# An mLSTM cell feeding a mixture-of-depths layer: score rows through DRAM, and four moves in the order of work

## The chip, the cores and the metric

The kernel runs on one core of a Trainium2 chip. The metric is the device time of one execution in microseconds (us), less is better. A core has a matrix engine (PE, whose weight loads are listed as PEld), a vector engine (DVE), an activation engine (ACT), a general engine (POOL) and a queue engine (SP) that issues transfers. They run side by side and wait for one another through semaphores; each takes its own instructions in the order of the program.

## What is computed

Cut to what matters, with B=4 batches, H=8 heads, S=768 tokens, D=40 (so 320 numbers per token) and capacity 128:

```
per token t of each batch and head:
    m_new = max(f[t] + m, i[t])
    C = exp(f[t] + m - m_new) * C + exp(i[t] - m_new) * outer(v[t], k[t])
    n = exp(f[t] + m - m_new) * n + exp(i[t] - m_new) * k[t]
    y[t] = sigmoid(o[t]) * (C @ q[t]) / max(|n . q[t]|, 1)
x = y as rows of 320
scores = x @ w_gate                        # one per token
out = x
per batch: top = the 128 tokens with the highest scores
    out[top] = x[top] + sigmoid(scores[top]) * (relu(x[top] @ w1) @ w2)
```

## The kernel before, in words

The recurrence is done in chunks of L=128 tokens: six chunks (NT=6) for each of four batches, 24 steps in all, `step(n)` (L615). Within a chunk the tokens meet as an attention-like product; a state C carries what came before. The stages of step n are spread over the engines and over neighbouring steps:

- SP loads k, q, v and the output gate of chunk n+4 (L119 to L133, each 160 KB in pieces of 160 bytes; there are five buffers of each).
- PE turns k and q of chunk n+2 (L308), makes the scores of chunk n+1 (pS, L363), the product with the state (pIC, L389 and L395), and for chunk n the weighted sum pH (L420). ACT copies the turned tiles (L309), makes the gate weights W (L342) and the output gate (L319, L320). POOL masks W (L347), scales v (L354), the state (L377) and the gate by the normalizer, sor (L435). DVE multiplies P = pS * W (L369), adds the state's part to pH (L425), forms the normalizer (L429 to L433) and the result x = pH * sor (L440), which SP stores to the output (L441).
- pH has one buffer in PSUM: PE can begin pH of step n+1 only when DVE has read pH of step n for x.

Then comes the selection. `score` (L443) takes the dot product of each token with w_gate on DVE; the scores of a chunk stand in one column, one per partition. To rank the tokens of a batch each score is compared with all others. For that `spread` (L449) brings the column to all partitions as a row: a PE transpose of the broadcast column (pb, L452) and an ACT copy (sb, L453). `compare(u)` (L455) then compares on DVE the scores of chunk u with those of chunks 0 to u and writes ge and a count. Before the change, step n spreads chunk n-1 in its middle and compares it at its end. The first step of a batch (c=0) and the very last step do both "soon", in the middle of the step; the prologue has scores 0 and 1 both made ahead of step 2, which therefore spreads and compares two.

After a batch's last comparison PE sums ge (pcol, L466), DVE turns sums and counts into ranks (L479, L480) and into a one-hot matrix sel (L484), PE makes token numbers of it (pidx, L491), DVE writes them as integers (idx, L496) and POOL gathers the 128 chosen rows from the output in DRAM (xe, L498). One step later PE turns these rows (pX, L514), and the two layers (L534, L543) are dealt out in portions over the steps of the next batch; `leave` (L545) scatters the results. For batch 0 the ranking is in step 7, the gather at the head of step 8 and pX in step 9. The last batch's selection is the tail after step 23 (L828 to L878).

The order on each engine is the order in which the program's lines run: nothing is moved by a scheduler. All loads and stores named above are on SP's one queue. At the start there are nine filler matmuls (`warm`, L183, on a tile of ones made by DVE at L92), which use PE while nothing else is ready; then come the column ends (pe, L201), the mask of the first weights (`masked`, L322), the running maxima (pm, L213) and the gate operands (pO, L269), and then the first chunk's turn and weights.

Two terms of the code: tiles of one `tag` in a pool share its `bufs` buffers, and a tile that is still in use keeps its buffer; `[(ps_h, "h"), (ps_c, "c")]` says where `masked` puts its two halves. `T` tiles come through the two buffers of `ps_t`.

Of the kernel before, what the change touches and what calls it, by code (L numbers as in the profile page):

```python
# [8 lines left out]
FP = mybir.dt.float32  # L9
BF = mybir.dt.bfloat16  # L10
# [11 lines left out]
def kernel(  # L22
# [20 lines left out]
    nc = tc.nc  # L43

    B, H, S, D = q.shape
    L = 128
    NT = S // L
# [19 lines left out]
    const = ctx.enter_context(tc.tile_pool(name="const", bufs=1))  # L67
# [5 lines left out]
    ps_t = ctx.enter_context(tc.tile_pool(name="ps_t", bufs=2, space=PSUM))  # L73
# [2 lines left out]
    ps_h = ctx.enter_context(tc.tile_pool(name="ps_h", bufs=1, space=PSUM))  # L76
    ps_m = ctx.enter_context(tc.tile_pool(name="ps_m", bufs=2, space=PSUM))


    NR = 3 * BH  # L80
    f_sb = [gate.tile([NR, L], FP, name=f"f_sb{g}") for g in range(2)]
# [6 lines left out]

    load_gates(nc.sync, f_sb, f_gate, 0)
    load_gates(nc.scalar, i_sb, i_gate, 0)  # L90
    fill = const.tile([128, 4 * L], BF, name="fill")
    nc.vector.memset(fill, 1.0)  # L92

    unused = const.tile([1, 1], FP, name="unused")
# [88 lines left out]
    def warm(n):  # L183

        pw = ps_c.tile([128, 4 * L], FP, name="pw", tag="c")
        for _ in range(n):
            nc.tensor.matmul(pw, fill[:, 0:128], fill, start=True, stop=True)  # L187

    def sums(g, eng):

# [131 lines left out]
    def masked(pools):  # L322

        pW = [pool.tile([128, 4, L], FP, name="pW", tag=tag) for pool, tag in pools]
        for p in pW:
            nc.tensor.matmul(p, never, ident_b.unsqueeze(1).to_broadcast([128, 4, L]), start=True, stop=False)
        return pW
# [87 lines left out]
    def within(P, v1):  # L415
        pH = ps_h.tile([128, H, DP], FP, name="pH", tag="h")
        for j in range(2):
            for p in range(NP):
                for t in HALVES:
                    nc.tensor.matmul(pH[t, 2 * p + j, :], P[:, p, j, t], v1[:, 2 * p + j, :], start=True, stop=True)  # L420
        return pH

    def norm(num, pH, so):
        if num is not None:
            nc.vector.tensor_tensor(out=pH[:, :, 0:D1], in0=num, in1=pH[:, :, 0:D1], op=OP.add)  # L425
        num = pH

        den = work.tile([128, H], FP, name="den")
        nc.vector.scalar_tensor_tensor(out=den, in0=num[:, :, D], scalar=-2.0, in1=twos.to_broadcast([128, H]),  # L429
                                       op0=OP.mult, op1=OP.max)  # L430
        nc.vector.scalar_tensor_tensor(out=den, in0=num[:, :, D], scalar=2.0, in1=den, op0=OP.mult, op1=OP.max)
        rec = work.tile([128, H], FP, name="rec")
        nc.vector.reciprocal(out=rec, in_=den)  # L433
        sor = work.tile([128, H, D], FP, name="sor", bufs=2)
        nc.gpsimd.tensor_tensor(out=sor, in0=so, in1=rec.unsqueeze(2).to_broadcast([128, H, D]), op=OP.mult)  # L435
        return num, sor

    def result(b, c, num, sor):
        x = x_t[b, c] = work.tile([128, DM], FP, name="x", bufs=NT)
        nc.vector.tensor_tensor(out=x.rearrange("p (h d) -> p h d", d=D), in0=num[:, :, 0:D], in1=sor, op=OP.mult)  # L440
        nc.sync.dma_start(out=out[b, c * L:(c + 1) * L, :], in_=x)  # L441
# [7 lines left out]
    def spread(u, sc, sb):  # L449

        pb = ps_m.tile([128, L], FP, name="pb", tag="m")
        nc.tensor.transpose(pb, sc[:, u:u + 1].to_broadcast([128, L]), ident)  # L452
        nc.scalar.copy(out=sb[:, u, :], in_=pb)  # L453

    def compare(u, sc, sb, ge, cnt):  # L455


        n = (u + 1) * L
        nc.vector.scalar_tensor_tensor(out=ge[:, GE[u]:GE[u + 1]], in0=sb.rearrange("p t l -> p (t l)")[:, 0:n],  # L459
                                       scalar=sc[:, u:u + 1], in1=earlier[:, NT * L - n:],  # L460
                                       op0=OP.is_ge, op1=OP.mult, accum_out=cnt[:, u:u + 1])
# [25 lines left out]
    def number(sel, token):  # L487

        pidx = ps_m.tile([K_, 1], FP, name="pidx", tag="m")
        for t in range(NT):  # L490
            nc.tensor.matmul(pidx, sel[:, t, :], token[:, t:t + 1], start=(t == 0), stop=(t == NT - 1))  # L491
        return pidx

    def gather(b, pidx):
        idx = mod.tile([K_, 1], U32, name="idx")
        nc.vector.tensor_scalar(out=idx, in0=pidx, scalar1=float(b * S), scalar2=None, op0=OP.add)  # L496
        xe = xe_t[b % 2]
        nc.gpsimd.indirect_dma_start(out=xe[0:K_, 0:DM], out_offset=None, in_=rows(b),  # L498
                                     in_offset=bass.IndirectOffsetOnAxis(ap=idx, axis=0),
                                     bounds_check=(b + 1) * S - 1, oob_is_err=False)  # L500
        return idx, xe
# [63 lines left out]
    N = len(steps)  # L565
    T, W, wv, state = {}, {}, {}, {}
    layers, sel, picked, x_t = {}, {}, {}, {}
    P, pS, nums = {}, {}, {}
    hidden = {0, 1, 2, 3}

    def load(n):
        if n < N:
            load_qk(n)
            load_v(n)
            load_so(n)
# [35 lines left out]
    def run(hooks):  # L611
        for f in hooks:
            f()

    def step(n, **more):  # L615
        b, c = steps[n]
        _, v1, so = loaded[n]
        pb, pc = steps[n - 1]
        load(n + AHEAD)
        pH = within(P[n], v1)  # L620
        if n == NT + 1:
            pcol = columns_of(state[0][1][2])
        elif n == NT + 2:
            picked[0] = gather(0, number(sel[0], token))
        elif n == NT + 3:
            enter(0)

        soon = c == 0 or n == N - 1
        if n + 1 < N:
            decay(*steps[n + 1])  # L630
            hide(n + 1)
            give = exchange(*steps[n + 1], loaded[n + 1][0], T[n + 1], wv[n + 1])
            if n + 1 not in pS:
                pS[n + 1] = products(T[n + 1])
        if soon:
            spread(pc, *state[pb][1][:2])
        if c == 0:
            state[b] = open_batch()

        num, sor = norm(nums.get(n), pH, so)  # L640
        if n + 1 < N:
            nums[n + 1] = exchanged(*steps[n + 1], *give)
            if n + 1 not in P:
                P[n + 1] = weighted(pS[n + 1], W[n + 1])
        if soon:
            if c == 0:
                result(b, c, num, sor)
            compare(pc, *state[pb][1])
        if n == NT + 1:
            ranked(0, pcol)  # L650
        if n + 2 < N:
            stated(n + 2)
        run(more.get("places", ()))
        if n < NT + 3:

            turned(n + 2)
            run(more.get("spread", ()))
            if not soon:
                spread(pc, *state[pb][1][:2])
            copies = operands(*((0, 5) if n == 2 else (1, n - 3)), [(ps_m, "m")])  # L660
            W[n + 2] = weights(*steps[n + 2])
            run(copies)
        else:
            if n + 2 < N:
                W[n + 2] = weights(*steps[n + 2])
                hide(n + 2)
            layer(b, c)
            if c == 1:
                picked[b - 1] = gather(b - 1, number(sel[b - 1], token))
            elif c == 2:  # L670
                enter(b - 1)
            if n + 2 < N:
                turned(n + 2)
            if c == 0:
                pcol = columns_of(state[b - 1][1][2])
            elif not soon:
                spread(pc, *state[pb][1][:2])
        if n + 2 < N:
            gated(n + 2)
        if c > 0:  # L680
            result(b, c, num, sor)
        score(b, c, state[b][0])
        run(more.get("end", ()))
        if not soon:
            compare(pc, *state[pb][1])
        if b > 1 and c == 0:
            ranked(b - 1, pcol)
        elif n == NT + 3 or (b > 1 and c == 2):
            layers[b - 1].gate()
            if b > 1:  # L690
                layers[b - 2].leave()
# [8 lines left out]
    load_so(AHEAD - 1)  # L700
    load(AHEAD)
    nc.sync.dma_start(out=wg, in_=moe_w_gate.rearrange("(o d) -> o d", o=1).to_broadcast([128, DM]))
    warm(9)

    sums(0, nc.vector)
    maxima(0)
# [1 line left out]
    for n in range(1, 4):  # L708
        pads(n, nc.gpsimd)
    ends(0)  # L710
    pW = masked([(ps_h, "h"), (ps_c, "c")])
    split(0, 0, nc.vector, slice(0, BH))
    carry(0)
    pm = carried(0)
# [73 lines left out]
    keep(1, columns(1))  # L788
    stated(3)
    score(0, 0, state[0][0])  # L790
    score(0, 1, state[0][0])

    def second_places():
        for j in range(2):
            nc.gpsimd.memset(place[j][1], 0.0)
        places(1)

    gated(3)
    step(2, places=[second_places], spread=[lambda: spread(0, *state[0][1][:2])],
         end=[lambda: compare(0, *state[0][1])])  # L800
    for n in range(3, N):
        step(n)
        if n == 3:
# [24 lines left out]
    b, u = steps[-1]  # L828
# [76 lines left out]
```

## Time and profile before

| | |
|---|---|
| time, median of 3 executions | 189.27 us (188.05 to 191.15) |
| profiled execution: own time, span from first to last instruction | 193.54 us, 191.8 us |
| PE, DVE, POOL, ACT busy | 179.0, 139.8, 101.4, 99.9 us |
| chain that ended last: PE, waiting for nothing shown, DVE, POOL, DMA | 65%, 11%, 11%, 7%, 3% |
| SP's transfers | 105008 pieces, 22.50 MB |

The share of busy time is an average over stages with different limits: up to about 24 us the start with its ramp, from 30 to 62 us a stretch where DVE has hardly a pause, 62 to 75 us the first ranking, 75 to 166 us PE without a pause, then the tail. The chain of waits goes back from the last instruction and names at each step what released it. "x8" after a line of the chain says how many instructions were merged.

### The profile page before, as it was taken

What the parts mean: (1) busy time and instruction counts of PE and PEld (TensorE: products, weight loads), DVE (VectorE), ACT (ScalarE), POOL (GpSimd) and SP (SyncE); (2) the same over time, 40 slices, a digit from 0 to 9 for tenths busy, and PEclk for the clock granted to TensorE, in tenths of its full rate; (3) what the DMA queues carried; (4) which work ended last, traced back from release to release, by engine and by line L of the source; (5) the groups of instructions that cost most, each with busy time, mean ns of one, the idle gap of its engine ahead of it and who ended that gap; (6) DMA issues with size and microseconds to landing.
All of it is one profiled execution on the core that took longest, in us unless ns stands there. A gap on an engine that the chain in (4) does not pass through costs nothing.

```text
span 191.8 us, 6510 instructions
## 1 busy us (share of the span) xinstructions
PE 179.0 (93%) x2594; PEld 149.8 (78%) x2594; DVE 139.8 (73%) x413; ACT 99.9 (52%) x233; POOL 101.4 (53%) x171
## 2 busy tenths in 40 slices
PE   6999999789999887999999999999999999989990
PEld 2577888677877775989878889798788898859960
DVE  7633748988999868867899778868997788585101
ACT  3054466589898678466734473567344734201110
POOL 7954356597676639413774657327746571023202
PEclk9999999999999999999999999999999999999999
DMA  4999996597998999999999498597993101010100
GB/s 79 140 156 148 145 171 100 108 173 151 198 223 180 164 224 251 170 172 183 159 172 143 98 166 152 104 188 120 147 127 83 39 34 38 36 38 36 34 0 34
DMA packets 105854, 24.37 MB, mean 127 GB/s; under 512 B 100640, under 2 KB 105248, under 8 KB 105824
## 3 DMA queue, kind: packets, MB, share of 16 engines
q1 hardware_dynamic: 105008, 22.50, 74.0%
q0 software_dynamic: 384, 1.31, 2.2%
q8 instruction: 20, 0.33, 0.8%
q10 hardware_dynamic: 432, 0.15, 0.7%
q14 instruction: 10, 0.08, 0.2%
HBM read 19.37 MB, written 4.59 MB: 125 GB/s over the span
## 4 chain that ended last, share of the span: by engine, by line
PE 65%; issue 11%; DVE 11%; POOL 7%; DMA 3%; ACT 1%; POOLq 1%; ACTq 0%
PE pS L363 11%; PE pH L420 10%; PE pt L308 10%; PE ph L534 9%; PE py L543 5%; PE pIC L389 4%; PE pIC L395 4%; PE pW L341 3%; DVE P L369 3%; POOL W L347 3%; PE pw L187 2%; DMA out_dram<-ye,idx 2%; DMA xe<-out_dram,idx 2%; DVE ge L459 1%; POOL sor L435 1%
## 5 line engine op out<-in xcount | busy, mean ns | idle before, releaser
L342 ACT ACTIVATE W<-pW 128x512 f32<-128x512 f32 x48 | 26.1, 595 | 24.6 <-PE pW L341 15.2
L435 POOL TENSOR_TENSOR sor<-so,rec 128x320 f32<-128x320 f32 x24 | 17.8, 740 | 39.1 <-DVE rec L433 32.8
L347 POOL TENSOR_SCALAR_AFFINE_SELECT W<-W 128x512 f32<-128x512 f32 x46 | 32.0, 718 | 10.9 <-ACT W L342 10.9
L369 DVE TENSOR_TENSOR P<-pS,W 128x512 f32<-128x512 f32 x48 | 30.9, 685 | 7.6 <-PE pS L363 3.7
L309 ACT COPY T<-pt 128x512 f32<-128x512 f32 x47 | 25.5, 589 | 20.0 <-PE pt L308 19.7
L420 PEld LDWEIGHTS pH<-v,P 128*64 128x64 f32 x768 | 24.9, 140 | 9.8 <-DVE x L440 5.5
L420 PE MATMUL pH<-v,P 128*64 128x64 f32 x768 | 28.1, 227 | 3.8 <-DVE x L440 2.4
L363 PE MATMUL pS<-T 64*128 64x128 f32 x384 | 29.7, 297 | 0.0
L308 PE MATMUL pt<-ident,qk 128*128 128x128 f32 x192 | 28.2, 294 | 0.0
L363 PEld LDWEIGHTS pS<-T 64*128 64x128 f32 x384 | 24.9, 199 | 2.5 <-issue 1.3
L459 DVE SCALAR_TENSOR_TENSOR ge<-sb,sc,earlier 128x128 bf16<-128x128 f32 (+5 forms) x23 | 17.5, 764 | 11.0 <-ACT sb L453 10.9
L308 PEld LDWEIGHTS pt<-ident,qk 128*128 128x128 f32 x192 | 23.3, 151 | 1.5 <-issue 0.2
L534 PE MATMUL ph<-xeT,w 128*128 128x128 f32 x192 | 23.8, 280 | 0.0
L534 PEld LDWEIGHTS ph<-xeT,w 128*128 128x128 f32 x192 | 22.1, 192 | 1.7 <-issue 1.6
L543 PE MATMUL py<-w,hT 128*128 128x320 f32 x64 | 19.3, 442 | 0.0
L354 POOL TENSOR_TENSOR wv<-v,cols 128x328 f32<-128x328 f32 x20 | 15.1, 756 | 5.4 <-DVE cols L284 5.4
L446 DVE CUSTOM_DVE_ANT_0 scr<-x,wg 128x320 f32<-128x320 f32 x24 | 15.7, 652 | 0.7
L543 PEld LDWEIGHTS py<-w,hT 128*128 128x128 f32 x64 | 11.5, 191 | 5.0 <-issue 1.4
L389 PE MATMUL pIC<-C,T 128*64 128x82 f32 x320 | 15.2, 236 | 0.0
L549 POOL DMA_INDIRECT out_dram<-ye,idx x4 | 4.6, 1144 | 19.4 <-DVE ye L547 19.4
L395 PE MATMUL pIC<-wv,qk 128*64 128x41 f32 x320 | 12.8, 230 | 0.7 <-POOL wv L354 0.7
L377 POOL TENSOR_TENSOR C<-C,cols 128x328 f32<-128x328 f32 x16 | 13.0, 810 | 0.2
(150 smaller groups left out, 265.4 us busy)
## 6 DMA issues: line engine op xcount, KB each, us to landing
qk<-in_k_dram SPq DMA_DIRECT2D x24, 160.0 KB, 4.4
qk<-in_q_dram SPq DMA_DIRECT2D x24, 160.0 KB, 4.8
v<-in_v_dram SPq DMA_DIRECT2D x24, 160.0 KB, 5.0
so<-in_o_gate_dram SPq DMA_DIRECT2D x24, 160.0 KB, 4.4
out_dram<-x SPq DMA_DIRECT2D x24, 160.0 KB, 2.0
w<-in_moe_w_dram SPq DMA_DIRECT2D x2, 640.0 KB, 5.8
w<-in_moe_w_dram SPq DMA_DIRECT2D x2, 512.0 KB, 4.6
w<-in_moe_w_dram SPq DMA_DIRECT2D x1, 256.0 KB
```

Source lines behind the costliest of these rows:

```text
L308: nc.tensor.transpose(pt[:, p, :], qk[:, j, 2 * p:2 * p + 2, :].rearrange("s a d -> s (a d)"), ident)
L309: copy(out=T[:, j], in_=pt)
L342: nc.scalar.activation(out=W[:, h0:h0 + 4, :], in_=pW, func=AF.Exp)
L347: nc.gpsimd.affine_select(out=W[:, h0:h0 + 4, :], in_=W[:, h0:h0 + 4, :], compare_op=OP.is_ge, fill=0.0, base=0, pattern=[[0, 4], [1, L]], ...
L363: nc.tensor.matmul(pS[j][:, p, :], T[e, 0, p, :], T[e, 1, p, :], start=True, stop=True)
L369: nc.vector.tensor_tensor(out=P[:, :, j, :], in0=pS[j], op=OP.mult, in1=W.rearrange("p (n a) t -> p n a t", a=2)[:, :, j, :])
L389: nc.tensor.matmul(pI[t, 2 * p * D1:2 * (p + 1) * D1], T[:, 1, p, t], C[:, p].rearrange("e a d -> e (a d)"), start=True, stop=True)
L395: nc.tensor.matmul(pC[e, p, :], qk[:, 0, 2 * p + j, :], wv[:, 2 * p + j, :], start=True, stop=True)
L420: nc.tensor.matmul(pH[t, 2 * p + j, :], P[:, p, j, t], v1[:, 2 * p + j, :], start=True, stop=True)
L435: nc.gpsimd.tensor_tensor(out=sor, in0=so, in1=rec.unsqueeze(2).to_broadcast([128, H, D]), op=OP.mult)
L534: nc.tensor.matmul(self.ph[:, f % 4, :], w1[:, j, f * 128:(f + 1) * 128], self.xeT[:, j, :], start=(j == 0), stop=(j == NDC - 1))
L543: nc.tensor.matmul(self.py, self.hT[:, f, :], w2[:, f, :], start=(f == 0), stop=(f == NFC - 1))
```

## The change

- `spread` is no longer called for chunks 0 to 4 of a batch (the last batch: 0 to 3). Instead, right after `score`, `store_row` writes the column of 128 scores as a row of 512 bytes into DRAM (128 pieces of 4 bytes), and at the next step, after the four loads of that step, `load_rows` reads this row back to all 128 partitions of sb (128 pieces of 512 bytes). Both are on SP's queue, and the second waits for the first to land. Chunk 5 of a batch, and the last two chunks of the last batch, are spread as before.
- `compare` of a chunk comes one step later: at the end of step c chunk c-2 is compared. At c=0 chunks 4 and 5 of the batch before are both compared, after x.
- In step 7 the result x comes in front of the ranking on DVE. In step 8 the gather comes behind `norm`, so behind sor (L435) on POOL; its idx comes behind the reciprocal on DVE.
- The fillers read one column of ones, broadcast. There are ten at the start, and two more behind `masked`, whose second half moves from `ps_c` to `ps_t`.

Instructions added and removed by engine: PE loses 19 transposes of 128x128 and gets 3 fillers, ACT loses 19 copies of 128x128, DVE and POOL keep theirs in another order, SP gets 38 transfers.

```diff
+    dram = ctx.enter_context(tc.tile_pool(name="dram", bufs=3, space=bass.MemoryType.DRAM))
-    fill = const.tile([128, 4 * L], BF, name="fill")
+    fill = const.tile([128, 1], BF, name="fill")
...
-            nc.tensor.matmul(pw, fill[:, 0:128], fill, start=True, stop=True)
+            nc.tensor.matmul(pw, fill.to_broadcast([128, 128]), fill.to_broadcast([128, 4 * L]), start=True, stop=True)
...
+    def store_row(n):
+        b, u = steps[n]
+        rows_of[n] = dram.tile([1, L], FP, name="row")
+        nc.sync.dma_start(out=rows_of[n].rearrange("o p -> p o"), in_=state[b][0][:, u:u + 1])
+    def load_rows(n):
+        b, u = steps[n]
+        nc.sync.dma_start(out=state[b][1][1][:, u, :], in_=rows_of.pop(n).to_broadcast([128, L]))
...
         load(n + AHEAD)
+        if n - 1 in rows_of:
+            load_rows(n - 1)
         pH = within(P[n], v1)
...
         elif n == NT + 2:
-            picked[0] = gather(0, number(sel[0], token))
+            pidx = number(sel[0], token)
...
         num, sor = norm(nums.get(n), pH, so)
+        if n == NT + 2:
+            picked[0] = gather(0, pidx)
...
                 result(b, c, num, sor)
+                compare(pc - 1, *state[pb][1])
             compare(pc, *state[pb][1])
         if n == NT + 1:
+            result(b, c, num, sor)
             ranked(0, pcol)
...
-            run(more.get("spread", ()))
-            if not soon:
-                spread(pc, *state[pb][1][:2])
...
-            elif not soon:
-                spread(pc, *state[pb][1][:2])
...
-        if c > 0:
+        if c > 0 and n != NT + 1:
             result(b, c, num, sor)
         score(b, c, state[b][0])
-        run(more.get("end", ()))
-        if not soon:
-            compare(pc, *state[pb][1])
+        if c < NT - 1 and n < N - 2:
+            store_row(n)
+        if c > 1:
+            compare(c - 2, *state[b][1])
...
-    warm(9)
+    warm(10)
...
-    pW = masked([(ps_h, "h"), (ps_c, "c")])
+    pW = masked([(ps_h, "h"), (ps_t, "t")])
+    warm(2)
...
     score(0, 0, state[0][0])
+    store_row(0)
+    load_rows(0)
     score(0, 1, state[0][0])
+    store_row(1)
...
-    step(2, places=[second_places], spread=[lambda: spread(0, *state[0][1][:2])],
-         end=[lambda: compare(0, *state[0][1])])
+    step(2, places=[second_places])
```

More of the change, by code (lines that the diff above doesn't have):

```diff
@@ L567 @@
     layers, sel, picked, x_t = {}, {}, {}, {}
-    P, pS, nums = {}, {}, {}
+    P, pS, nums, rows_of = {}, {}, {}, {}
     hidden = {0, 1, 2, 3}
```

## The prediction, made before the changed kernel was run

> **What bounds the kernel now.** I read the busy slices first, then the chain of waits, then the timelines of SP and DVE around the places that the change touches. Busy shares and transfers by slice (40 slices of 4.8 us; a DMA digit is the mean share of 16 transfer engines):
>
> ```profile
> span 191.8 us, 6510 instructions
> ...
> PE   6999999789999887999999999999999999989990
> ...
> DVE  7633748988999868867899778868997788585101
> ...
> DMA  4999996597998999999999498597993101010100
> ```
>
> PE is full from 75 to 166 us; before that DVE is the fuller one (slices 6 to 12), and the transfers are at 9 in most slices up to 105 us. The chain of waits has four lines that matter here:
>
> ```profile
> 7.92 1.90 PE pt L308 x8
> ...
> 59.15 0.87 PE pt L308 x8
> ...
> 65.32 4.48 issue
> ...
> 82.32 0.11 PE pb L452
> ```
>
> The same eight transposes take 1.90 us at 7.92 and still at 21.48, but 0.87 later: PE runs at half speed until about 24 us (pH at 23.39 takes 1.56, later 1.08). The 4.48 us are POOL standing at the first gather. A pb costs PE 0.11 us.
>
> The timeline of SP's queue in the DVE stretch (start, time to issue):
>
> ```profile
> 34.60 0.39 SPq L121 DMA_DIRECT2D qk<-in_k_dram  x1
> ...
> 37.64 0.68 SPq L121 DMA_DIRECT2D so<-in_o_gate_dram  x1
> 39.60 0.36 SPq L441 DMA_DIRECT2D out_dram<-x  x1
> ...
> 42.04 2.07 SPq L121 DMA_DIRECT2D so<-in_o_gate_dram  x1
> 45.57 0.36 SPq L441 DMA_DIRECT2D out_dram<-x  x1
> ...
> 56.72 0.68 SPq L121 DMA_DIRECT2D so<-in_o_gate_dram  x1
> 57.49 1.79 SPq L441 DMA_DIRECT2D out_dram<-x  x1
> ```
>
> SP has little to spare: it waits for x only 1.28 us before 39.60, 1.46 before 45.57 and 0.47 before 50.73, and then issues without a pause until past 90 us. By the single transfers' rows, the so of 42.04 lands after 4.5 us, that of 56.72 after 4.0 us; an x store lands 1.9 us after 39.60, but 5.2 us after 63.50, behind the loads in the queue. DVE where chunk 5 is compared:
>
> ```profile
> 60.20 0.48 DVE L440 TENSOR_TENSOR x<-pH,sor 128x320 f32<-128x320 f32 x1
> 60.60 1.01 DVE L459 SCALAR_TENSOR_TENSOR ge<-sb,sc,earlier 128x768 bf16<-128x768 f32 x1
> 61.53 0.08 DVE L459 DVE_READ_ACCUMULATOR ge<-sb,sc,earlier 128x1 f32 x1
> 61.53 0.91 DVE L446 CUSTOM_DVE_ANT_0 scr<-x,wg 128x320 f32<-128x320 f32 x1
> ...
> 62.38 0.49 DVE L425 TENSOR_TENSOR pH<-num,pH 128x328 f32<-128x328 f32 x1
> ```
>
> **What the Trainium skill says.** "TensorE: Matmul & The Clock Gate", Part 1: PE starts at half clock and gets the full one after a busy window of about 3.4 us, and these windows run freely, so the moment differs between executions. The trace agrees on the two speeds; but PE was busy from 1.53 to 9.82 and stayed slow until 24, so which work counts is open. "DMA: Bandwidth & Descriptors", Two DMAs through the same engine are not ordered: a transfer that reads what another wrote must wait for that one's completion. The same page, Issuing engines are not separate DMA queues: all issuers end on the same 16 engines. The 5.2 us of an x store behind loads fits that. The same page, Specifications, says that pieces under 512 bytes are written by read-modify-write; no 4-byte store to DRAM is in this trace.
>
> **Part 1, the start.** Nine fillers took 4.02 us, 0.447 each. The smaller fill (a 128x1 memset takes 0.06 us, L164; the old one 0.48) lets them begin 0.42 earlier, the tenth ends it at 5.58 instead of 5.55: nothing. The two new ones stand between the masks (end 6.93) and pm: +0.89 at slow clock. And with one half of the mask in `ps_t`, q's turn must take the buffer of k's turn: it waits for DVE's copy (0.69), +0.8 with the semaphore. Slow clock: +1.7. But the unbroken run of PE work at the start grows from 5.40 us (1.53 to 6.93) to 6.8 us (1.11 to 7.87), with the six tiny pe products (0.41) in it. A window of 3.41 us lies wholly inside with chance (5.40-3.41)/3.41 = 58% before, near all after. If it counts, PE is fast from about 7.3 us: the chain's PE work from 7.17 to 24.95 is 17.4 us and would be 9.2 at later durations. It can't save 8.2, since other engines then stand in the chain. Walked through with the trace's durations: first turn with its two copies to 10.6, W 11.7, pS 11.7, P 13.1, operand copy 13.8, second W 15.4 and its mask 16.7, P 18.0, level and operand copy 19.4; there pW was at 24.88. So -5.4, say -5.3 with the costs above contained. I give the fast start 0.75 after the change. The spread of before (188.05 to 191.15, and 193.54 profiled) I read as this moment moving; its median has most of the gain already.
>
> **Part 2, the rows.** Removed: 19 pb, of which 12 lie in the PE-bound stretch: 12 x 0.11 = -1.3. The ACT copies (19 x 0.28) are off the path there. DVE waited 10.9 us in total for sb, 8.9 of it between 75 and 160 us where PE is the bound, so worth nothing by itself.
> Added: 38 transfers on SP. A row store costs 0.4 us of SP (as the x store, 0.36) and lands after 1.9 us on an empty queue, about 5 behind loads; bounds: 0 if hidden, 5 if waited for. In the prologue nothing hides it. Store 0 waits for score 0 (DVE to 36.12), load 0 for its landing (38.1), then come store 1 and only then load k of step 2: 39.1 instead of 34.60. Thus +4.5 on SP. Its pauses give back 1.28 + 1.46 + 0.47 = 3.2, the six row transfers up to step 5 take 6 x 0.4 = 2.4: at step 5 SP is 3.7 late. By landings instead: from 46.56 to 60.70 came eight loads at 1.1 us (160 KB at 145 GB/s, window 62 to 66), two x, and two weights of 640 KB at 276 GB/s (window 66 to 70), 8.8 + 0.5 + 4.6 = 13.9 of 14.1 us. No slack there, so 4.5 less the first two pauses plus 0.8 for the rows and a lost start is up to 4.9. I take 4.3 (between 0.5 and 8).
> Row 4 is loaded behind step 5's so, which landed at 60.70: it lands at 60.70 + 0.4 + 4.3 = 65.4. DVE asks for it after x at 60.6 (compare 4 now stands there). Behind it on DVE are compare 5, the score, and pH of step 7, for which POOL's sor, x and PE's next pH wait. 65.4 + 0.9 + 1.0 + 0.6 = 67.9 against 62.38: +5.5. Chunks 1 to 3 wait less, inside this.
> At later batches c=0 DVE has compare 4 more (0.9) in front of pcol, which PE reached just as ge was ready (100.11 and 100.43): +0.5 at each of two, +1.0. In the tail compare 3 now stands between the last score and the counts, +0.75, and the earlier wait for sb (pH could start 0.25 sooner) is gone: +0.5.
>
> **Part 3, steps 7 and 8.** x before rank and sel (0.16 + 0.16 + 0.96): PE's pH of step 8 no longer waits for them, -1.2. The gather behind sor lets state, mask and sor run on POOL while idx is made: x of step 8 about 0.9 sooner. Together -2.1; but the gather is issued about 0.7 later, lands 4.0 after issue, and pX then waits about 0.6. Net -1.5.
>
> **Sum.** 193.54 - 5.3 + 5.5 - 1.5 - 1.3 + 1.0 + 0.5 = 192.4 with a fast start. Against the best of before, which I take for a fast start: 188.05 + 1.7 + 4.2 = 194.0. The walk thus overstates by some; I take 193.6, +2.3% on the median 189.27. About 2% is what a measurement of this kernel can tell from no change (185.5 to 193.1).
>
> **Rivals.**
> A, the forecast: rows late, start fast, 193.6, own range 190.5 to 196.5: 0.50.
> A2: rows late, start slow. 193.54 + 1.7 + 4.2 = 199.4: 0.15. For it: 5.40 us of work did not suffice in the profiled execution.
> B, the other side: the rows land before DVE asks. The place is compare 4 in step 6, the price 5.5; it decides if row 4 lands by 60.6, that is, if SP makes up its 4.5 us through a shallower queue. For it: windows at 56 to 62 us show transfers at 0.75, not full. Against: x at 57.49 took 1.79 to issue. 193.6 - 5.5 = 188.1, same: 0.25.
> C: as B, and the freed ACT and DVE waits count in the DVE stretch: 188.1 less 3.6 (a third of the 10.9), 184.5: 0.10. Against: the chain has no sb wait there.
> Loads so late that the steps run dry would add to A: v of chunk 12 had some 3 us to spare; that is the upper end.
>
> **Chances.** Slower: A2 0.15 and 0.32 of A, 0.47. Same: 0.18 of A, 0.23 of B, 0.41. Faster: C and 0.02 of B, 0.12. The range leaves out part of C and of A2: 186.8 to 199.8.
>
> **What would show it.** After: eight pt at about 0.9 us near 9 us (start right) or 1.9 (A2). k of step 2 on SP some 4.5 us behind the second x store. A DVE wait "ge <- DMA sb<-row" of about 4 us at the first c=0 step, and some in steps 4, 5 and 8. No pb in the steady steps. A gap at pcol in steps 12 and 18. If no such ge wait stands in the DVE stretch, A is wrong and B holds; if PE is fast at 9 us and the time is still above 197, loads were the cause.

## The result, and the profile after

The changed kernel takes 302.72 us (median of four executions, 300.98 to 303.84) against 190.21 us for the kernel before, measured beside it: a ratio of 1.604, with a 95% interval of 1.585 to 1.622. The forecast was 193.6 us with a range up to 199.8. In the runs below the kernel before takes 188.4 to 192.0 us. The ratios leave out executions more than 1.5% above the fastest of their kernel; the profiled execution of before, 193.54 us with PE at half clock until 24 us, is such a one.

First the busy slices of the changed kernel (40 slices of 7.6 us) and its costliest group, with the idle time ahead of it:

```profile
span 302.1 us, 6514 instructions
...
PE   8898917637224989119832997965505999804993
...
DVE  7578423532405753038144585505225587115310
...
PEclk9999966775855799857875799795955999955598
DMA  7999368798979876968949975665859821312000
...
L471 DVE SCALAR_TENSOR_TENSOR ge<-sb,sc,earlier 128x128 bf16<-128x128 f32 (+5 forms) x23 | 15.2, 668 | 121.2 <-DMA sb<-row 121.2
```

The kernel before had no such holes in PE and DVE between its start and its tail. Now DVE stands 121.2 us at the comparison, waiting for a row that a transfer brings. The table of waits says that this is 17 waits, the longest 17.0 us. The granted clock of PE falls again and again after the holes; its mean is 0.79.

Where the row comes from is seen in the timeline of SP's queue (start, time to issue), at the place of the prologue where before the k of step 2 was issued at 34.60:

```profile
29.23 2.08 SPq L443 DMA_DIRECT2D out_dram<-x  x2
31.40 0.38 SPq L461 DMA_DIRECT2D row<-sc  x1
39.70 0.33 SPq L465 DMA_DIRECT2D sb<-row  x1
40.12 0.38 SPq L461 DMA_DIRECT2D row<-sc  x1
40.59 0.38 SPq L123 DMA_DIRECT2D qk<-in_k_dram  x1
...
43.28 5.57 SPq L123 DMA_DIRECT2D so<-in_o_gate_dram  x1
```

The first row store goes out at 31.40. The load of this row can't go before the store has landed: 39.70, that is 8.30 us later. Only then come store 1 and k. And the loads behind store 1 are slow as well: the so at 43.28 takes 5.57 us to issue, where so took 0.68 at 37.64 before. In the single transfers' rows q and v of 41.03 and 41.70 land 9.3 and 9.5 us after issue; over the whole run v lands after 9.5 us (median), where before it was 5.0.

The table by stretches shows what the 16 transfer engines do meanwhile (columns: stretch, length, busy time of PE, PEld, DVE, ACT, POOL with counts, clock, DMA share, GB/s):

```profile
24.00:31.40 7.40, 6.01 (x126) 5.24 (x125) 6.39 (x18) 4.51 (x11) 4.84 (x7) 1.00 1.12 160
31.40:39.70 8.30, 7.06 (x112) 5.21 (x109) 2.28 (x8) 7.05 (x17) 5.31 (x13) 1.00 0.15 38
...
41.00:49.00 8.00, 1.97 (x36) 1.97 (x38) 4.41 (x14) 0.94 (x3) 2.39 (x8) 0.50 1.09 56
```

While the lone store is under way the transfer engines are nearly idle (0.15): it isn't work that fills them, it is one landing that doesn't come. With loads queued behind the next store they are all "busy" (1.09) and move 56 GB/s, where they moved 160 at about the same share (1.12) before the store. The share of busy time doesn't tell transfers that flow from transfers that stand.

The chain of waits goes through these places one after the other:

```profile
31.40 8.24 DMA row<-sc
...
39.70 3.19 DMA sb<-row
...
42.92 0.36 DVE ge L471 x2
...
60.62 4.29 DMA sb<-row
```

Store, load, compare, and later again the load of a row: each step waits for its row. The x of successive steps stand at 46.50, 56.06, 68.39 and 82.92 in the timeline of DVE, 10 to 15 us apart, where before they were 5 to 6 apart.

The start did what was foreseen, as the head of the chain of the changed kernel shows:

```profile
7.50 0.60 PE pt L310 x4
8.87 0.66 PE pt L310 x4
10.30 1.09 PE pS L365 x16
```

The eight transposes are 1.26 us and the 16 products 1.09; in the profiled execution of before they were 1.90 and 2.01. A later product of the start, the pW behind the first step's pH, begins at 18.65 instead of 24.95.

### The profile page after: what moved, and what is told of

The parts are those of the page before. It is cut to its first block, busy times and chain, and to the rows that moved or that the text cites. A ratio compares the mean times of both kernels' runs of the same rounds, so it can differ in the third digit from the quotient of the medians.

```text
span 302.1 us, 6514 instructions
## 1 busy us (share of the span) xinstructions
PE 196.3 (65%) x2578; PEld 163.2 (54%) x2578; DVE 134.5 (45%) x413; ACT 96.7 (32%) x214; POOL 97.9 (32%) x171
## 4 chain that ended last, share of the span: by engine, by line
PE 32%; DMA 21%; issue 14%; SPq 13%; DVE 10%; POOL 7%; ACT 1%; POOLq 1%
DMA sb<-row 14%; SPq L123 12%; PE pH L422 6%; DMA row<-sc 6%; PE pS L365 5%; PE pt L310 4%; PE pIC L391 3%; DVE ge L471 3%; POOL W L349 3%; PE ph L546 3%; PE pIC L397 3%; PE py L555 2%; DVE P L371 2%; PE pw L189 2%; POOL sor L437 2%
## 5 line engine op out<-in xcount | busy, mean ns | idle before, releaser
L471 DVE SCALAR_TENSOR_TENSOR ge<-sb,sc,earlier 128x128 bf16<-128x128 f32 (+5 forms) x23 | 15.2, 668 | 121.2 <-DMA sb<-row 121.2
L422 PE MATMUL pH<-v,P 128*64 128x64 f32 x768 | 33.9, 253 | 32.2 <-DVE x L442 22.2
L422 PEld LDWEIGHTS pH<-v,P 128*64 128x64 f32 x768 | 30.3, 164 | 39.7 <-DVE x L442 26.3
L478 PE MATMUL pcol<-ones_b,ge 128*128 128x1 bf16 x78 | 2.9, 166 | 48.0 <-DVE ge L471 48.0
L349 POOL TENSOR_SCALAR_AFFINE_SELECT W<-W 128x512 f32<-128x512 f32 x46 | 29.4, 663 | 11.9 <-ACT W L344 11.4
L365 PE MATMUL pS<-T 64*128 64x128 f32 x384 | 31.9, 311 | 1.2 <-issue 1.2
L478 PEld LDWEIGHTS <-ge 128*128 128x128 bf16 x78 | 2.5, 105 | 49.3 <-DVE ge L471 49.3
L555 PE MATMUL py<-w,hT 128*128 128x320 f32 x64 | 21.7, 485 | 0.0
L391 PE MATMUL pIC<-C,T 128*64 128x82 f32 x320 | 18.7, 269 | 0.0
L391 PEld LDWEIGHTS pIC<-C,T 128*64 128x64 f32 x320 | 15.9, 164 | 0.4 <-POOL W L349 0.2
L397 PE MATMUL pIC<-wv,qk 128*64 128x41 f32 x320 | 14.7, 247 | 0.7 <-POOL wv L356 0.7
```

Of the source, the lines that this page charges most:

```text
L349: nc.gpsimd.affine_select(out=W[:, h0:h0 + 4, :], in_=W[:, h0:h0 + 4, :], compare_op=OP.is_ge, fill=0.0, base=0, pattern=[[0, 4], [1, L]], ...
L365: nc.tensor.matmul(pS[j][:, p, :], T[e, 0, p, :], T[e, 1, p, :], start=True, stop=True)
L391: nc.tensor.matmul(pI[t, 2 * p * D1:2 * (p + 1) * D1], T[:, 1, p, t], C[:, p].rearrange("e a d -> e (a d)"), start=True, stop=True)
L555: nc.tensor.matmul(self.py, self.hT[:, f, :], w2[:, f, :], start=(f == 0), stop=(f == NFC - 1))
```

## Experiments

Theory W: the store itself is the cause. 128 pieces of 4 bytes next to one another in DRAM land late and hold up the transfers behind them. Rival L: the load, or the order store, landing, load on SP's queue. Rival S: the other parts of the change (start, later compare, moved gather) carry a good part of the loss. Where a result has a ratio with an interval, its time is a median of several executions; the others are single executions. They come from several chips, on which the kernel before takes 188.4 to 192.0 us, so between single executions a difference of up to about 4 us tells nothing.

**1. No rows.** All of the change but the row transfers; PE and ACT spread all scores in the places of before.

```diff
-        if n - 1 in rows_of:
-            load_rows(n - 1)
...
+            if n == 2:
+                spread(0, *state[pb][1][:2])
+            if not soon:
+                spread(pc, *state[pb][1][:2])
...
-        if c < NT - 1 and n < N - 2:
-            store_row(n)
```

> The changed kernel without its row transfers: the scores of all chunks are spread by PE and ACT in the places of the kernel before, the rest of the change (start, later compare, gather behind the gate scaling, x in front of the ranking) stays. Theory R (all of the loss is in the row transfers): 183 to 190 us, since the prediction's other terms sum to -5.3 - 1.5 + 1.0 + 0.5 = -5.3 on the profiled execution of before. Rival S (the later compare or the moved gather stalls DVE or POOL too): above 195.

Measured: 194.27 us, ratio 1.035 (1.029 to 1.041). So 108 of the 113 us lost are in the rows (302.7 - 194.3), and the rest is not the gain that was forecast but a loss of 3.5%. The time lies between the two brackets: theory R of the expectation (all of the loss is in the rows) is right in the main, and S on a small remainder, which experiments 5 to 8 take up.

**2. Stores only.** As 1, with the 19 row stores put back and read by nobody.

```diff
         score(b, c, state[b][0])
+        if c < NT - 1 and n < N - 2:
+            store_row(n)
...
+    store_row(0)
     score(0, 1, state[0][0])
+    store_row(1)
```

> As the kernel without row transfers, with the 19 row stores put back and no row load: nobody reads what they write (the scores reach all partitions through PE as before). Theory W (the store is the cause: it holds the transfer engines about 8 us each time, and the loads behind it): 19 x 5 to 8 us on a transfer-bound kernel, 260 to 300 us, a store lands about 8 us after its issue and the loads of q and v behind it take 9 instead of 5. Rival L (the cause is the chain store, landing, load on SP's queue, or the load): under 200, stores land in about 2 us.

Measured: 271.3 us, in the bracket of theory W. The stores alone cost 77.0 us over the kernel without rows, 4.05 each, though nothing waits for what they write. What waits is the work behind the loads that were issued after a store, as the chain of waits shows:

```profile
32.88 11.75 DMA qk<-in_q_dram
...
45.51 9.92 DMA qk<-in_k_dram
```

In the kernel before these loads land after 4.8 and 4.4 us (medians). Rival L can't be the main cause.

**3. Loads only.** As 1, with 19 loads of the same form, reading 128 numbers of the gate vector into a spare tile.

```diff
-        nc.sync.dma_start(out=state[b][1][1][:, u, :], in_=rows_of.pop(n).to_broadcast([128, L]))
+        nc.sync.dma_start(out=mod.tile([128, L], FP, name="spare"), in_=moe_w_gate[0:L].rearrange("(o d) -> o d", o=1).to_broadcast([128, L]))
```

> As the kernel without row transfers, with the 19 row loads alone, in their places behind the four loads of a step: they read 128 numbers of the gate vector into a tile that nobody uses, so they wait for no store. Theory W: within 3 us of the kernel without row transfers (19 x 64 KB at 145 GB/s is 0.45 us each, 8 us only if transfers bind all the way). Rival L (reading one 512-byte row 128 times is the slow part): over 250.

Measured: 195.0 us, 0.7 more than without. Reading one row 128 times costs nothing that can be told here.

**4. Stores to separate lines.** As 2, each number to a row of its own.

```diff
-        rows_of[n] = dram.tile([1, L], FP, name="row")
-        nc.sync.dma_start(out=rows_of[n].rearrange("o p -> p o"), in_=state[b][0][:, u:u + 1])
+        rows_of[n] = dram.tile([L, L], FP, name="row")
+        nc.sync.dma_start(out=rows_of[n][:, 0:1], in_=state[b][0][:, u:u + 1])
```

> As the store-only kernel, but each of the 128 numbers of a store goes to a row of its own, 512 bytes from the next, instead of all into the same 512 bytes. Theory W1 (writes of 4 bytes into the same stretch of DRAM wait for one another, 128 x 0.064 us = 8.2 us): the store lands in 2 to 3 us here and the kernel takes under 205. Theory W2 (a 4-byte write is slow wherever it goes): a store still takes 8 us and the kernel is as slow as the store-only one.

Measured: 194.8 us against 271.3. The same number of 4-byte pieces, the same bytes, the same places on the queue; only the distance between the addresses differs. The stores land after 2.9 us (median). SP's timeline shows both first stores and k behind them without a pause:

```profile
31.26 0.89 SPq L461 DMA_DIRECT2D row<-sc  x2
32.25 0.38 SPq L123 DMA_DIRECT2D qk<-in_k_dram  x1
```

The so behind them takes 0.88 us to issue, at 33.99; in experiment 2 it takes 6.60, at 36.76. So it isn't the smallness of the pieces, it is that they are neighbours (W1).

**5. The start alone,** in the kernel before.

```diff
-    fill = const.tile([128, 4 * L], BF, name="fill")
+    fill = const.tile([128, 1], BF, name="fill")
...
-            nc.tensor.matmul(pw, fill[:, 0:128], fill, start=True, stop=True)
+            nc.tensor.matmul(pw, fill.to_broadcast([128, 128]), fill.to_broadcast([128, 4 * L]), start=True, stop=True)
...
-    warm(9)
+    warm(10)
...
-    pW = masked([(ps_h, "h"), (ps_c, "c")])
+    pW = masked([(ps_h, "h"), (ps_t, "t")])
+    warm(2)
```

> The kernel before with the start of the change alone (fillers from one column, ten and two of them, half of the mask in the other buffer). The kernel without row transfers was 3.5% slower than before, though its start ran 6.3 us ahead of the profiled execution of before. Theory G (the loss is in the gather stage and the later compare; the start gains, or the other executions of before have an early clock too): 184 to 189 us. Rival S (the lead of the start is what runs into the loads, and the loss comes with it): 192 to 195.

Measured: 189.39 us, ratio 0.999 (0.995 to 1.003): nothing that can be told. In the traces of experiments 6, 7 and 8, which have the start of before, the eight transposes near 7.4 us take 1.09 or 1.10 us in PE's timeline: there PE is at full clock as early. The half-clock start of the profiled execution is the exception, and against the median there was nothing to gain. Whether the new start does away with starts like the profiled one's is not settled: of the 39 executions of before that stand beside these 20 three took over 193.5 us, as the profiled one did, and of the 20 none took over 192.7, which is too few to tell.

**6. x first and the gather moved,** in the kernel before.

```diff
-            picked[0] = gather(0, number(sel[0], token))
+            pidx = number(sel[0], token)
...
+        if n == NT + 2:
+            picked[0] = gather(0, pidx)
...
+            result(b, c, num, sor)
             ranked(0, pcol)
...
-        if c > 0:
+        if c > 0 and n != NT + 1:
             result(b, c, num, sor)
```

> The kernel before with x in front of ranking in step 7 and the gather behind the gate scaling in step 8, nothing else. The prediction has -1.5 us: 186 to 188. Rival (PE waits for the gathered rows with nothing else to do, in the kernel without row transfers 2.86 us ahead of pX, and then runs four to five us at half clock): 191 to 195.

Measured: 191.36 us, ratio 1.010 (1.006 to 1.014): in the bracket of the rival, and slower where -1.5 us was forecast.

**7. The later compare,** in the kernel before.

```diff
             if c == 0:
                 result(b, c, num, sor)
+                compare(pc - 1, *state[pb][1])
             compare(pc, *state[pb][1])
...
-        if not soon:
-            compare(pc, *state[pb][1])
+        if c > 1:
+            compare(c - 2, *state[b][1])
```

> The kernel before with each compare one step later, two of them at c=0, nothing else. The prediction has +1.0 in steps 12 and 18 and +0.5 in the tail: 189.5 to 191. Rival (the two compares at c=0 hold up everything behind x on DVE, in the kernel without row transfers 2.20 us of compares right behind x at 98.20): 192 to 195.

Measured: 191.54 us, ratio 1.013 (1.001 to 1.024), between the two brackets. The forecast's +1.5 us for steps 12, 18 and the tail is 0.8%, inside the interval.

**8. x first alone.** The edit of 6 without the gather's.

> The kernel before with x in front of the ranking in step 7 alone; with the gather behind the gate scaling too it was 1.0% slower. If the prediction's -1.2 us for this part is right and the moved gather is what loses: 186.5 to 188.5. If this part loses (sel is late by x, 0.4 us, and with it the gather and pX): 190 to 191.5.

Measured: 189.84 us beside 189.02, between the two brackets. The ratio is 0.993 (0.990 to 0.997), but it comes from 7 of the 22 executions and 16 of the 27 of before, and the medians of all executions point the other way. So the -1.2 us of the forecast for x is neither shown nor refuted. Nor is the price of the moved gather: between this kernel and that of experiment 6 lie 1.7% by the ratios, some 3 us, and 0.6% by the medians, some 1 us, and no run moves the gather alone.

What the traces show is PE's wait for the gathered rows. PE's timeline of the kernel without rows (idle time and its releaser in brackets):

```profile
67.14 1.15 PE L422 MATMUL pH<-v,P 128*64 128x64 f32 x32
71.15 0.87 PE L526 MATMUL pX<-ident,xe 128*128 128x128 f32 x3 [2.86 <-DMA xe<-out_dram,idx]
```

and its chain of waits just behind:

```profile
74.14 2.01 PE pS L365 x16
...
76.68 3.89 PE ph L546 x18
```

PE has nothing queued ahead of pX that it could do. It waits 2.86 us for the gathered rows, and the following work runs at half speed: pS takes 2.01 us instead of 1.09, ph 3.89 instead of 2.21. The kernel with x first and the gather moved has the same wait in its trace, and 4.14 us for the same 18 ph. But the half speed is not the moved gather's alone. With x first alone PE pauses 1.10 and 1.24 us just before pX, and then:

```profile
72.56 2.01 PE pS L363 x16
...
75.10 2.73 PE ph L534 x18
```

The two profiled executions end these ph at 77.8 us (x first alone) and 78.3 (with the gather moved), so they don't show where 1 or 3 us would come from. The Trainium skill, "TensorE: Matmul & The Clock Gate", HAM oscillation, warns of PE's waits for transfers that bring the clock down and puts them above about 3.4 us; in these traces the half speed followed a wait of 2.86 us, and in another two pauses of 1.10 and 1.24 us.

The three parts together give 0.999 x 1.010 x 1.013 = 1.021, and the kernel of experiment 1 is at 1.035. The other 1.4% may come from the parts together or from noise: the interval of experiment 7 alone reaches 1.024. No run takes that apart.

**9. One piece.** PE turns the score column into one partition (1x128), ACT copies it, and the row goes to DRAM as one piece of 512 bytes in the middle of the next step, with its load right behind.

```diff
+        pb = ps_m.tile([1, L], FP, name="pb", tag="m")
+        nc.tensor.transpose(pb, state[b][0][:, u:u + 1], ident)
+        line = mod.tile([1, L], FP, name="line")
+        nc.scalar.copy(out=line, in_=pb)
         rows_of[n] = dram.tile([1, L], FP, name="row")
-        nc.sync.dma_start(out=rows_of[n].rearrange("o p -> p o"), in_=state[b][0][:, u:u + 1])
+        nc.sync.dma_start(out=rows_of[n], in_=line)
```

> The changed kernel with the row made by PE: a transpose of the score column to one partition (1x128), an ACT copy, then one piece of 512 bytes to DRAM in the middle of the next step, and the row read back to all partitions as before. It keeps the way through DRAM and takes away the 128 small pieces. Theory W1 (the 4-byte pieces into one stretch are the whole cause): the store lands in 2 to 5 us, no long wait of ge for a row, 194 to 200, as the kernel without row transfers plus up to 5. Rival L (store and load after each other on one queue cost on their own): over 220.

Measured: 225.88 us, ratio 1.188 (1.176 to 1.201). Theory W1 as the whole cause is missed, and the number of rival L came true: the small pieces are gone and it is still 31.6 us slower than without rows. The table of SP's own waits says where:

```profile
SPq L469 <- DMA row<-line: 32.0, 18, 2.7
SPq L465 <- ACT line L463: 28.3, 7, 6.7
```

SP stands at 18 of the 19 loads until their store has landed (1.8 us on the mean, 2.7 at most) and at seven stores until ACT has made the line, and all of the next step's loads stand behind it. So the way of the row, store, landing, load on the queue that feeds the kernel, has a price of its own, which the prediction counted once and not 19 times. Here the store stands closer to the load than in the change, so the size is this kernel's.

**10. Where the rest of the rows' loss is.** Row stores and loads in the places of the change, the loads into a spare tile; scores through PE.

```diff
-        nc.sync.dma_start(out=state[b][1][1][:, u, :], in_=rows_of.pop(n).to_broadcast([128, L]))
+        nc.sync.dma_start(out=mod.tile([128, L], FP, name="spare"), in_=rows_of.pop(n).to_broadcast([128, L]))
```

> The changed kernel with its row stores and loads in their places, the loads into a tile that nobody uses; the scores come through PE as before. It splits the 31 us between the store-only kernel (271.3) and the changed one (302.7). If they are DVE's waits for the rows: 271 to 278. If SP standing at the load until the store has landed is what costs, with all loads behind it: 295 to 303.

Measured: 297.9 us. From 271.3 (stores only) to 297.9 is the load that waits on SP's queue for the landing, 26.6 us. From there to 302.7 are 4.8 us, little more than what lies between chips: what DVE's waits for rows add, less the 19 transposes and copies that only the kernel of this experiment does. The 121 us that the profile puts on ge are mostly not what the kernel would gain if nobody waited for a row: the loads of k, q, v and so are late anyway.

**11. The whole change with separate lines.** Stores as in 4 (into three fixed areas of 64 KB filled with constants), the load reads the first line of the area: one score and constants. Order, waits and bytes of the rows are the change's; POOL also clears the two tiles for gathered rows whole instead of their rims, once.

```diff
+    lines = [dram.tile([L, L], FP, name=f"lines{j}", bufs=1) for j in range(3)]
+    for x in lines:
+        nc.gpsimd.dma_start(out=x, in_=ident)
...
-        rows_of[n] = dram.tile([1, L], FP, name="row")
-        nc.sync.dma_start(out=rows_of[n].rearrange("o p -> p o"), in_=state[b][0][:, u:u + 1])
+        rows_of[n] = lines[n % 3]
+        nc.sync.dma_start(out=rows_of[n][:, 0:1], in_=state[b][0][:, u:u + 1])
...
-        nc.sync.dma_start(out=state[b][1][1][:, u, :], in_=rows_of.pop(n).to_broadcast([128, L]))
+        nc.sync.dma_start(out=state[b][1][1][:, u, :], in_=rows_of.pop(n)[0:1, :].to_broadcast([128, L]))
```

> The changed kernel with each of the 128 numbers written 512 bytes from the next, and the load reading the first of these rows, one score and constants, so it still waits for the store and moves as much, but the selection is not the reference's. Theory W1: no more than the row's way with an ordinary landing of about 3 us, 197 to 210 (194.8 for the stores alone, and up to 15 for the loads that wait for them). If the chain store, landing, load costs on its own whatever the landing takes, as the kernel with one piece (225.9) suggests: 215 to 230.

Measured: 209.0 us. The first load goes 2.11 us behind its store (37.30 and 39.41 in SP's timeline). With an ordinary landing the rows cost 14.7 us over the kernel without rows; the late landing, with what stands behind it, is the other 93.7.

**12. A row in SBUF.** As the change, but the row is a tile on one partition.

```diff
-        rows_of[n] = dram.tile([1, L], FP, name="row")
-        nc.sync.dma_start(out=rows_of[n].rearrange("o p -> p o"), in_=state[b][0][:, u:u + 1])
+        rows_of[n] = mod.tile([1, L], FP, name="row", bufs=3)
+        nc.sync.dma_start(out=rows_of[n], in_=state[b][0][:, u:u + 1])
...
-        nc.sync.dma_start(out=state[b][1][1][:, u, :], in_=rows_of.pop(n).to_broadcast([128, L]))
+        nc.sync.dma_start(out=state[b][1][1][:, u, :], in_=rows_of.pop(n).unsqueeze(1).to_broadcast([1, 128, L]))
```

> The changed kernel with the row in SBUF on one partition instead of in DRAM: the same 128 pieces of 4 bytes into the same 512 bytes, the same load to all partitions, the same places on SP's queue. Theory W1 for DRAM alone: the store lands in 2 to 3 us, no long wait of ge, 198 to 215. If small writes into one 512-byte stretch of SBUF wait for one another as well: about 300.

Measured: 214.6 us; the first load goes 2.03 us behind its store (32.12 and 34.15), stores land after 3.5 us (median). The same 128 neighbouring pieces don't land late in SBUF. The 214.6 is 20 us above the kernel without rows; the order store, landing, load made 14.7 of experiment 11, and the rest is not taken apart.

**13. How near is too near.** Stores only, read by nobody, 64 bytes apart, and, with 4 for 16 columns, 16 bytes apart.

```diff
-        rows_of[n] = dram.tile([1, L], FP, name="row")
-        nc.sync.dma_start(out=rows_of[n].rearrange("o p -> p o"), in_=state[b][0][:, u:u + 1])
+        rows_of[n] = dram.tile([L, 16], FP, name="row")
+        nc.sync.dma_start(out=rows_of[n][:, 0:1], in_=state[b][0][:, u:u + 1])
```

> The store-only kernel with the 128 numbers of a store 64 bytes apart (16 columns of 4 bytes, the first is written): eight of them lie in each 512 bytes. It asks how wide the stretch is in which small writes wait for one another. If it is 64 bytes or less: about 195 us, stores land in 3, like the kernel with rows of 512 bytes. If it is 512 bytes: eight in line at 64 ns each, 16 such rows side by side or not: 195 to 210. If the whole 8 KB counts as one: 270.

> The store-only kernel with the 128 numbers of a store 16 bytes apart, four in each 64 bytes and 32 in each 512. It asks how wide the stretch is within which small writes wait. If 512 bytes: each such stretch takes 32 numbers at 0.064 us, 2 us more, four side by side or 8 us one after another: 215 to 270. If 64 bytes: four at 0.064 is 0.2 us and stretches run side by side: 193 to 198. If the whole 2 KB is one stretch: about 270.

Measured: 193.0 us at 64 bytes, where stores land in 2.5 us (median); 200.4 us at 16 bytes, 4.0 us. With four neighbours in 64 bytes a price begins (6.1 us over the kernel without rows, 0.3 for each store), with sixteen it is 77.0. At 64 bytes, eight in each 512 bytes, there is none. A wait within 512-byte stretches, 32 numbers at 0.064 us, would have made the landing of 16-byte distance 2 us later; it is 1.5 later than at 64 bytes. So the stretch itself isn't settled: its price grows between 64 and 4 bytes of distance.

**14. Does the price go with the number?** Half of the column, stores only; and, because no landing is on record there, half and a quarter of the column with the lone first store of the change ahead of its load (the kernel of 10).

```diff
-        nc.sync.dma_start(out=rows_of[n].rearrange("o p -> p o"), in_=state[b][0][:, u:u + 1])
+        nc.sync.dma_start(out=rows_of[n][:, 0:L // 2].rearrange("o p -> p o"), in_=state[b][0][0:L // 2, u:u + 1])
```

> The store-only kernel with half of the column, 64 numbers next to one another in 256 bytes. If each of the pieces waits for the one before at 0.064 us, the first store lands after about 4.1 us plus what a landing takes otherwise, 4.5 to 5.5 in all, and the kernel lies midway between 194 and 271, at 220 to 240. If the wait is a fixed price of any such store: 265 to 271.

> The kernel whose rows are stored and loaded but read by nobody, with 64 instead of 128 numbers in each row. Its first store stands alone before its load, as in the changed kernel, where 128 numbers took 8.24 us. If the price goes with the pieces (0.064 us each): 4.1 to 5 us. If it goes by stretches or by engines, or is fixed: 7 to 8.5 us, as the 257.3 us of the half-column stores with nobody reading suggest (3.3 us each against 4.05 for whole ones).

> The same with 32 numbers in each row, 128 bytes. If the price goes with the pieces: the first store takes 2.1 to 3.5 us and the kernel is near 215. If it is fixed: 7 to 8.5 us, and over 280.

Measured: 257.3 us for the half stores (62.9 us, 3.3 each, against 4.05 for whole ones; between the two brackets), and 277.7 and 246.4 us for half and quarter with their loads (297.9 for the whole). From SP's timelines, the first store and its load with 128 numbers:

```profile
31.81 0.38 SPq L461 DMA_DIRECT2D row<-sc  x1
39.45 0.33 SPq L465 DMA_DIRECT2D spare<-row  x1
```

with 64:

```profile
32.24 0.51 SPq L461 DMA_DIRECT2D row<-sc  x1
39.90 0.33 SPq L465 DMA_DIRECT2D spare<-row  x1
```

with 32:

```profile
31.61 0.40 SPq L461 DMA_DIRECT2D row<-sc  x1
35.94 0.33 SPq L465 DMA_DIRECT2D spare<-row  x1
```

That is 7.64, 7.66 and 4.33 us. The 0.064 us for each piece, with which several of the expectations reckon, is refuted: half the pieces take as long. Nor is the price fixed: a quarter takes 3.3 us less, which falls in neither bracket. By what rule it grows stays open.

## Why the prediction was wrong

**The row store: the step that failed.** "A row store costs 0.4 us of SP (as the x store, 0.36) and lands after 1.9 us on an empty queue, about 5 behind loads; bounds: 0 if hidden, 5 if waited for." The 0.4 of SP was right (0.38). The landing took 8.2 us with the transfer engines nearly idle (0.15). The bound was taken from the nearest row, an x store, whose 128 pieces are whole rows of 1280 bytes. A store of 4-byte neighbours was known not to be in the trace, and the bound should have been open upwards. The prediction cited the Trainium skill, "DMA: Bandwidth & Descriptors", Specifications, for the read-modify-write of pieces under 512 bytes, and gave it no number. That this is the mechanism is argued, not shown: 4-byte pieces 64 bytes apart fall under the same sentence and land in 2.5 us. What the runs show is that distance decides.

**What stands behind the store.** The step priced the store by who waits for its row. The larger part, 77.0 of 108 us, is paid with nobody waiting: loads that share the 16 engines stand behind it. The sentence of the skill ("DMA: Bandwidth & Descriptors", Issuing engines are not separate DMA queues) that all issuers end on the same engines was cited for the 5.2 us of an x store, and not turned round: that a slow store holds up the loads, as with the 11.75 us of experiment 2.

**SP's queue.** k of step 2 was forecast 4.5 us behind the second x store; it is 10.2 behind (30.39, the second of the merged pair, to 40.59). The sum then let SP's pauses absorb the lateness. They could not: a store in every step makes it anew. In the sum by landings the two x stores, 160 KB each, stand with 0.5 us together; at the 276 GB/s that it takes for the weights they are 1.2, which only strengthens its "No slack there".

**The stall at ge.** "+5.5" once, in step 6. It comes 17 times. "A DVE wait of about 4 us" has the right place and releaser, and the mechanism of rival A, rows late, was the right one. Its frequency was missed because the row was treated as late by the prologue's 4.3 us alone; also with an ordinary landing (experiment 11) the rows cost 14.7 us where the sum had +5.5 - 1.3, so the landing alone would not have put the forecast right.

**Clock.** That the holes would bring PE's clock down (mean 0.79) wasn't in the sum. How many of the 113 us it makes isn't measured by itself.

**The start.** The early clock was forecast with 0.75 and is there in the trace. Its -5.3 holds only against the profiled execution (pW at 18.65 instead of 24.95); "its median has most of the gain already" was right: against the median no gain is left, ratio 0.999.

**Third part.** Together forecast -1.5, measured +1.0% (0.6 to 1.4), some 2 us. The term that failed is "pX then waits about 0.6", which is 2.86. How much of the rest belongs to x and how much to the gather stays open (experiment 8).

**Later compare.** Forecast +1.5 in all, measured +1.3% (0.1 to 2.4): the sign was right, the size fits within a wide interval. "No pb in the steady steps": right, and worth nothing where PE is no longer the bound.

**Rivals.** A2 is wrong, since the start had the early clock, and so are B and C, since the rows came late. "If PE is fast at 9 us and the time is still above 197, loads were the cause" named what happened but not why: the steps do run dry for late loads, which the prediction had as its upper end, and experiment 2 shows that the stores make the loads late. The row loads themselves cost nothing that can be told (experiment 3).

No version with rows through memory beat the kernel before, and of the other moves none was shown to gain.

## What to carry to other kernels

Don't write a column of single numbers to neighbouring addresses in DRAM: here 128 of them took 8.2 us to land and held up the transfers behind them, at 4 us each time; at 64 bytes apart they cost nothing that could be told (193.0 us against 194.3). Why the distance decides is not shown. A transpose of 0.11 us and a copy of 0.28 that look wasteful on busy engines can be the cheap way when the other way puts a store, its landing and a load into the queue that feeds the kernel. And a bound taken from the nearest row holds only if what makes the row different, here piece size and distance, is known to be free; if not, measure it alone before it is summed.

## What the runs showed of the hardware

- From the issue of a lone store of neighbouring 4-byte pieces to DRAM to that of the load that waits for it, 128 and 64 pieces take the same time, 7.6 and 7.7 us, and 32 pieces 4.3; 128 pieces 512 bytes apart take 2.1, and 128 neighbours into SBUF 2.0.
- Transfer engines can be "busy" at 1.09 and move 56 GB/s. The share has to be read with the GB/s.
- A PE wait of 2.86 us before pX was followed by work at half clock (pS 2.01 us instead of 1.09, then part of the 3.89 us of ph); two pauses of 1.10 and 1.24 us, with 1.15 us of work between them, were followed by it as well (pS 2.01).
- With the same start, executions differ in when PE gets its full clock: about 24 us in the profiled one of the kernel before, by 7.4 in the three traces of experiments 6, 7 and 8. The clock row of the kernel before shows nothing of it (mean 1.000); the durations do (eight transposes 1.90 us, later 0.87).
